# An attention and two-layer MoE kernel: another order of the opening's hand-written plan, and the first transposes in another PSUM bank

## The chip, the cores and the metric

The kernel runs on one core of a Trainium2 chip. The metric is the device time of one execution in microseconds (us), and the number quoted for a kernel is the median of its runs. Five engines matter: PE (matrix products, with PEld loading its weights), DVE and ACT (elementwise work, reductions and activations), POOL (hardly used), and SP, which issues the transfers (DMAs). Each engine works through its own instruction list strictly in the order in which the program wrote it; engines wait for each other through semaphores.

## The reference

```python
scores = scale * np.matmul(q_c, k_c.transpose(0, 1, 2, 4, 3))      # blocks of 64 tokens, 8 heads
attn = np.exp(scores - np.max(scores, axis=-1, keepdims=True))
attn = attn / (np.sum(attn, axis=-1, keepdims=True) + 1e-09)
x = (attn @ v_c), heads joined                                       # 2304 tokens x 512
h = x @ w_in;   g = h * (1.0 / (1.0 + np.exp(-1.702 * h)));          x = g @ w_out   # 512 -> 2048 -> 512
h = x @ w_in2;  g = h * np.tanh(log1p(exp(h)));                      return g @ w_out2
```

So there are three stages: chunked attention with a softmax over blocks of 64 keys, then two feed-forward layers. The weights arrive as 64-bit floats, and the kernel makes 32-bit numbers of them itself.

## The kernel before

**Tiling.** The 2304 tokens are 18 attention tiles of 128 tokens. Three tiles make a block of 384 tokens, and a block is what the first layer's in-projection takes as its moving operand. The hidden width of 2048 is cut into 16 steps of 128. Step n of a block has an in-projection, called `I` n here (`in_proj`, 12 matmuls of 128x384 into a bank `h`), a GELU on ACT, a split of its result into a high and a low part, and an out-projection, called `O` n (`out_a`, 12 matmuls into the banks `acc0` and `acc1`). Each product of 32-bit accuracy is three matmuls of rounded parts: high weight x high x, high weight x low x, low weight x high x (`mm3`, lines 354 to 356). The third matmul of a product therefore is the first that reads the low part of the weight.

**The weights of the first layer.** There are 32 weight tiles, numbered in the order of use: in-weights i0, i1, then o0, i2, o1, i3, o2, i4 and so on, so in-weight n is number 2n-1. During the first 16 steps each is loaded by SP and then converted in four operations on two engines: a scale on ACT (`c`, line 196), a join of the two 32-bit words on DVE (`j`, lines 200 and 201), a cast to the high part on ACT (`s`, line 155), and the subtraction that makes the low part on DVE (`rest`, line 163). In the second and later blocks the converted weights lie in memory and are used again.

**What sets the order.** The scheduler is switched off: instructions stand in each engine's list in the order in which the program emits them. For the first block's attention (tiles 0 to 2), the fourth tile's attention up to its normalisation, in-projections 0 to 3 and out-projections 0 and 1, a string of steps named `PLAN` (line 24) gives that order, one letter per step: `T` transposes of q and k, `Q K` copies out of PSUM, `S` scores, `M` maximum and subtraction, `X` exp, `N` sums, `U` normalisation, `A` transposes of the weights of attention, `V` its copy, `P` the product with v, `H L` the high and low part of x, `I` in-projection, `G Y Z` GELU and its parts, `O` out-projection, `l` a weight load, `d v` loads of tokens, `w` a number of idle matmuls that only keep PE busy, and `c j s` as above. After it a plain loop (line 748) runs from step 4. In each of its first 12 turns it emits a piece of a later tile's attention, the in-projection, a call of `convert`, the GELU and its high part, the out-projection of two steps back, and `convert` again. One `convert` (line 171) emits one cast, one join, the pending low parts and one scale, each for the next tile in line. The attention piece in turns 7 and 12 is scores, shift, exp, sums and normalisation. How far the conversions are ahead of the in-projections in the loop is set by how many of them `PLAN` holds.

**Banks.** `usual` and `every` (lines 619 and 620) are lists of PSUM tags that an attention tile takes in turn; the first three tiles go round `at`, `acc0` and `acc1`. The tag `h` has two buffers; the idle matmuls write one of them, and the in-projections then take them in turn.

Of the kernel before, what the change touches and what calls it, by code (L numbers as in the profile page):

```python
# [9 lines left out]
F32 = mybir.dt.float32  # L10
# [6 lines left out]
P = 128  # L17
# [4 lines left out]


PLAN = """
    w8 d0 d1 w8 T0 T1 w1 Q1 k0 K1 d2 q0 S0 M0 l S1 X0 T2 l v2 M1 N0 K2 l Q2 X1 S2 U0 c N1 c
    M2 j w17 l v0 A0 X2 N2 V0 c c j j v1 l U1 U2 A1 V1 P0 A2 d3 P1 s H0 V2 c w2 H1 s L0 P2 s
    T3 j H2 d4 K3 L1 Q3 s L2 c j I0 G0 s c j s S3 I1 Y0 G1 c Y1 Z0 M3 j Z1 c s c I2 G2 j s
    Y2 I3 c j O0 Z2 j X3 N3 s U3 s j G3 c s Y3 c O1 Z3 j
"""
BF16 = mybir.dt.bfloat16  # L30
PSUM = bass.MemoryType.PSUM
# [4 lines left out]
def tile_kernel(  # L36
# [17 lines left out]
    nc = tc.nc  # L54
# [18 lines left out]
    ident = const.tile([P, P], F32, name="ident")  # L73
# [9 lines left out]
    def wslot(tag, shape, dtype, name):  # L83
        pool = early_w if FREED.index(tag) < SOON else late_w
        return pool.tile(shape, dtype, tag=tag, name=name)


    class Weights:
# [54 lines left out]
        def join(self):  # L143
            if (i := self._next("join")) is None:
                return
            self.f32[i] = join_raw(self.raw.pop(i))

        def split(self):
            if (i := self._next("split")) is None:
                return  # L150
            key = kind, f = self.order[i]
            w = self.f32.pop(i)
            both = wslot(f"w{kind}{f}", [P, 2, DM], F32R, f"w{kind}{f}")
            hi, lo = both[:, 0], both[:, 1]
            nc.scalar.copy(hi, w)
            self.hi[key] = hi
            self.open.append((key, w, hi, lo))
# [72 lines left out]
    class Attention:  # L230
# [77 lines left out]
            rc = self.rc.to_broadcast([P, G, CH])  # L308
            eng.tensor_tensor(out=self.eg, in0=self.eg, in1=rc, op=ALU.mult)

        def attn_t(self):
            self.pt = self.psum("at")
            for p in range(NP):
                s = slice(p * P, (p + 1) * P)
                nc.tensor.transpose(self.pt[:, 0, s], self.e[:, s], ident)

        def take_a(self, copy):
            if self.a is None:
                self.a = at.tile([P, DM], F32, tag="k", name=f"a{self.i}")
            copy(self.a, self.pt[:, 0, :])  # L320

        def pv(self):
            self.pt = pt = self.psum("pv")
# [285 lines left out]
    ps = ctx.enter_context(tc.tile_pool(name="ps", bufs=2, space=PSUM))  # L609
# [7 lines left out]
    with tc.manual_schedule():  # L617
        at, ps_at = at_cm.__enter__(), ps_at_cm.__enter__()
# [7 lines left out]
        tiles = dict(enumerate(first))  # L626
# [4 lines left out]
        w1 = W[0]  # L631
# [26 lines left out]
        def join():  # L658
# [9 lines left out]
            "c": lambda _: w1.scale(),  # L668
            "j": lambda _: join(),
            "s": lambda _: split(),  # L670
            "T": lambda i: tiles[i].transposes(),
            "Q": lambda i: tiles[i].take("q", act),
            "K": lambda i: tiles[i].take("k", act),
# [4 lines left out]
            "X": lambda i: tiles[i].exp(),  # L678
            "N": lambda i: tiles[i].sums(),
            "U": lambda i: tiles[i].normalize(nc.vector),  # L680
            "A": lambda i: tiles[i].attn_t(),
            "V": lambda i: tiles[i].take_a(act),
            "P": lambda i: tiles[i].pv(),
            "H": lambda i: tiles[i].x_hi(act),
# [63 lines left out]
        for n in range(4, NA):  # L748
            f = n % KF
# [25 lines left out]
            j = n // KF  # L775
# [142 lines left out]
        G2 = {}  # L918
# [25 lines left out]
        for p in range(PAIRS):  # L944
# [78 lines left out]
            for i, (k, c) in enumerate(units):  # L1023
                name = OUT[k]
# [65 lines left out]
```

## Time and profile before

| what | value |
|---|---|
| median of 3 runs | 847.68 us (847.05 to 847.93) |
| the profiled execution | 848.96 us, of which the span is 847.1 us |
| PE busy | 826.9 us (98%), 6228 instructions |
| DVE busy | 551.8 us (65%), 1059 instructions |
| ACT busy | 394.3 us (47%), 710 instructions |
| DMA, q1 | 120064 packets, 179.33 MB, 66.6% |
| mean granted clock of PE | 0.995 |

The page's slices, 21 us each, show where PE is not full: 6 tenths in the first, 8 in the second, 9 or more in nearly all others. The chain that ended last is 85% PE. The shares of the other engines are averages; in the opening DVE (5, 7, 9, 8, 7 tenths) and ACT (3, 7, 9, 8, 6 tenths) are far busier than later. The profiled execution took 1.28 us more than the median of the runs, and its span ends 1.86 us short of its own time.

### The profile page before, as it was taken

The numbers are of one execution on the slowest core, as the hardware profiler recorded it, in microseconds if no ns is written. First come the engines' busy times: TensorE is split into PE (matmuls) and PEld (weight loads), VectorE is DVE, ScalarE is ACT, GpSimd is POOL, SyncE is SP. The second block draws the span as 40 slices with busy tenths as digits, with TensorE's granted clock in tenths as the row PEclk, the third lists the DMA queues.
The fourth block names the chain that finished last, engine by engine and source line by source line (L and its number), as shares of the span: only waits on it lengthen the run. The fifth ranks groups of instructions, "written<-read, shape, count | busy, mean of one in ns | idle before, by whom it ended". The sixth has DMA issues, their size and how long they took to land.

```text
span 847.1 us, 15662 instructions
## 1 busy us (share of the span) xinstructions
PE 826.9 (98%) x6228; PEld 804.9 (95%) x6228; DVE 551.8 (65%) x1059; ACT 394.3 (47%) x710; POOL 0.7 (0%) x6
## 2 busy tenths in 40 slices
PE   6899999999999999999999999999999999999998
PEld 4799899999999999999999999999999999999998
DVE  5798757657676766766525466678556687566664
ACT  3798644445544443545212333356333365333442
POOL 0000000000000000000000000000000000000000
PEclk9899999999999999999999999999999999999999
DMA  9867634747667673864445278788888778877761
GB/s 245 269 189 242 176 113 142 207 155 242 176 199 216 172 230 130 250 173 163 164 149 224 87 246 301 250 269 259 249 312 275 263 243 262 273 253 236 256 199 56
DMA packets 120135, 180.31 MB, mean 213 GB/s; under 512 B 61440, under 2 KB 82432, under 8 KB 120064
## 3 DMA queue, kind: packets, MB, share of 16 engines
q1 hardware_dynamic: 120064, 179.33, 66.6%
q8 instruction: 49, 0.80, 0.4%
q14 instruction: 22, 0.18, 0.1%
HBM read 140.51 MB, written 38.80 MB: 212 GB/s over the span
## 4 chain that ended last, share of the span: by engine, by line
PE 85%; DVE 7%; ACT 3%; DMA 3%; SPq 1%; issue 1%; DVEq 0%
PE sum_acc L887 14%; PE sum_y L857 11%; PE h L857 9%; PE h L354 7%; PE acc L355 7%; PE acc L356 7%; PE acc L354 7%; PE h L355 7%; PE h L356 7%; PE sum_y L887 5%; DMA raw<-in_moe_w_out_dram 1%; PE tr L258 1%; DVE raw L201 1%; PE sc L275 1%; PE pv L330 1%; SPq L224 1%
## 5 line engine op out<-in xcount | busy, mean ns | idle before, releaser
L354 PE MATMUL h<-xh,wi 128*128 128x384 f32 x384 | 134.9, 351 | 0.0
L355 PE MATMUL acc<-gl,wo 128*128 128x384 f32 x384 | 129.2, 337 | 1.8 <-DVE gl L380 1.8
L356 PE MATMUL h<-xh,wi 128*128 128x384 f32 x384 | 129.1, 336 | 1.8 <-DVE wi L163 1.8
L355 PE MATMUL h<-xl,wi 128*128 128x384 f32 x384 | 129.2, 336 | 0.5 <-DVE xl L350 0.5
L356 PE MATMUL acc<-gh,wo 128*128 128x384 f32 x384 | 129.1, 336 | 0.0
L354 PE MATMUL acc<-gh,wo 128*128 128x384 f32 x384 | 129.1, 336 | 0.0
L372 ACT ACTIVATE t<-h 128x384 f32<-128x384 f32 x96 | 47.0, 490 | 125.4 <-PE h L356 100.0
L376 DVE CAST gh<-t 128x384 fp32r<-128x384 f32 x80 | 28.8, 360 | 90.2 <-ACT t L372 90.2
L355 PEld LDWEIGHTS acc<-gl,wo 128*128 128x128 f32 x384 | 72.2, 188 | 2.4 <-DVE gl L380 2.4
L356 PEld LDWEIGHTS h<-xh,wi 128*128 128x128 f32 x384 | 72.2, 188 | 2.1 <-DVE wi L163 2.1
L354 PEld LDWEIGHTS h<-xh,wi 128*128 128x128 f32 x384 | 72.2, 188 | 2.0
L355 PEld LDWEIGHTS h<-xl,wi 128*128 128x128 f32 x384 | 72.4, 188 | 0.8 <-DVE xl L350 0.8
L356 PEld LDWEIGHTS acc<-gh,wo 128*128 128x128 f32 x384 | 72.2, 188 | 0.0
L354 PEld LDWEIGHTS acc<-gh,wo 128*128 128x128 f32 x384 | 72.2, 188 | 0.0
L380 DVE TENSOR_TENSOR gl<-t,gh 128x384 fp32r<-128x384 f32 x96 | 53.5, 557 | 5.5 <-ACT gh L376 2.7
L867 ACT ACTIVATE v<-h 128x384 f32<-128x384 f32 x24 | 11.9, 494 | 61.9 <-PE h L857 60.3
L926 DVE TENSOR_TENSOR v<-u,sum_y 128x384 f32<-128x384 f32 x24 | 13.3, 553 | 31.7 <-PE sum_y L857 31.7
L926 DVE TENSOR_TENSOR g_a<-u,sum_y 128x384 f32<-128x384 f32 x24 | 13.3, 553 | 31.0 <-PE sum_y L857 31.0
L867 ACT ACTIVATE g_a<-g_a 128x384 f32<-128x384 f32 x24 | 12.6, 525 | 40.8 <-DVE g_a L926 40.8
L867 ACT ACTIVATE v<-v 128x384 f32<-128x384 f32 x24 | 12.6, 524 | 35.2 <-DVE v L926 35.2
L926 DVE TENSOR_TENSOR g_s<-v,g_s 128x384 f32<-128x384 f32 x48 | 26.8, 558 | 0.8
L461 DVE TENSOR_TENSOR s<-raw2i,s 128x512 fp32r<-128x512 f32 (+1 forms) x32 | 19.9, 621 | 10.8 <-ACT s L460 10.8
(499 smaller groups left out, 1841.0 us busy)
## 6 DMA issues: line engine op xcount, KB each, us to landing
fs<-w_sums SPq DMA_DIRECT2D x84, 512.0 KB, 4.6
fb_p<-w_out_sums SPq DMA_DIRECT2D x60, 512.0 KB, 4.4
w_sums<-s SPq DMA_DIRECT2D x24, 512.0 KB, 2.6
fa<-w_outs SPq DMA_DIRECT2D x24, 512.0 KB, 4.7
raw<-in_moe_w_in_dram SPq DMA_DIRECT2D x16, 512.0 KB, 5.8
raw<-in_moe_w_out_dram SPq DMA_DIRECT2D x16, 512.0 KB, 5.5
raw2i<-in_moe_w_in_dram SPq DMA_DIRECT2D x16, 512.0 KB, 4.6
raw2o<-in_moe_w_out_dram SPq DMA_DIRECT2D x16, 512.0 KB, 5.2
```

The costliest lines, as they stand in the source:

```text
L201: nc.vector.scalar_tensor_tensor(hi, hi, 3, lo, op0=ALU.logical_shift_left, op1=ALU.bitwise_or)
L354: nc.tensor.matmul(o, wh, mh, start=start, stop=False)
L355: nc.tensor.matmul(o, wh, ml, start=False, stop=False)
L356: nc.tensor.matmul(o, wl, mh, start=False, stop=stop)
L372: nc.scalar.activation(gt[n], hp.pop(n), AF.Gelu_apprx_sigmoid)
L376: (nc.scalar.copy if n < KF else nc.vector.tensor_copy)(gh[n], gt[n])
L380: nc.vector.tensor_tensor(out=gl[n], in0=gt.pop(n), in1=gh[n].bitcast(F32), op=ALU.subtract)
L461: nc.vector.tensor_tensor(out=lo, in0=w, in1=hi.bitcast(F32), op=ALU.subtract)
L857: nc.tensor.matmul(h, t[:, u, which, ks], moving[:, kk], start=start and kk == 0 and i == 0, stop=kk == 1 and i == 2, skip_group_check=not ...
L867: nc.scalar.activation(t, c, AF.Mish)
L887: nc.tensor.matmul(o, gs[a][:, ts], w[:, b], start=start and i == 0 and t != 1, stop=stop and i == 2, skip_group_check=again or t > 0,)
L926: nc.vector.tensor_tensor(out=out, in0=x, in1=h, op=op)
```

## The change

The plan is written in another order, and three other edits come with it. The step `A` of the plan (tiles 0 to 2) no longer takes the next tag of its tile's list but a bank of the tag `h`, handed to it as an argument (the loop still calls it without one). A step `r` is new: it emits the pending low parts of weights. One `PLAN` line of each side stands for the string:

```diff
-    w8 d0 d1 w8 T0 T1 w1 Q1 k0 K1 d2 q0 S0 M0 l S1 X0 T2 l v2 M1 N0 K2 l Q2 X1 S2 U0 c N1 c
+    w8 d0 d1 w8 T0 T1 w1 Q1 k0 K1 d2 q0 S0 M0 l S1 X0 T2 v0 M1 N0 K2 l Q2 X1 S2 U0 v1 l v2
...
-        def attn_t(self):
-            self.pt = self.psum("at")
+        def attn_t(self, bank=None):
+            self.pt = self.psum("at")[:, 0, :] if bank is None else bank
             for p in range(NP):
                 s = slice(p * P, (p + 1) * P)
-                nc.tensor.transpose(self.pt[:, 0, s], self.e[:, s], ident)
+                nc.tensor.transpose(self.pt[:, s], self.e[:, s], ident)
...
-            copy(self.a, self.pt[:, 0, :])
+            copy(self.a, self.pt)
...
+            "r": lambda _: w1.rest(),
...
-            "A": lambda i: tiles[i].attn_t(),
+            "A": lambda i: tiles[i].attn_t(ps.tile([P, 512], F32, tag="h", name=f"at{i}")),
```

Counted in the two strings: before, 13 `c`, 12 `j` and 11 `s`; now 10, 9 and 8. All else is there equally often but for the idle matmuls, `l` (5, now 7) and `r` (none, now 1).

**PE, tiles 0 to 2 and the first in-projection.** `at` is the transposes of step `A`, `pv` step `P`, `tr3` the fourth tile's `T`, `h0` in-projection 0; rows of idle matmuls are left out. Before:

```order
L315 MATMUL at0_276<-ident_72,e0_172 128x128 x4
L315 MATMUL at1_301<-ident_72,e1_209 128x128 x4
L330 MATMUL pv0_308<-a0_287,v0_274 64x64 x16
L315 MATMUL at2_325<-ident_72,e_first_106 128x128 x4
L330 MATMUL pv1_336<-a1_306,v1_295 64x64 x16
...
L330 MATMUL pv2_384<-a_first_107,v2_207 64x64 x16
L258 MATMUL tr3_403<-ident_72,q3_330 128x128 x4
L258 MATMUL tr3_403<-ident_72,k3_332 128x128 x4
L354 MATMUL h0_439<-xh0_373,wi0_353 128x384
```

Now:

```order
L315 MATMUL at0_251<-ident_72,e0_172 128x128 x4
L330 MATMUL pv0_271<-a0_259,v0_205 64x64 x16
...
L315 MATMUL at1_294<-ident_72,e1_207 128x128 x4
L330 MATMUL pv1_319<-a1_307,v1_241 64x64 x16
...
L315 MATMUL at2_340<-ident_72,e_first_106 128x128 x4
L330 MATMUL pv2_350<-a_first_107,v2_245 64x64 x16
L354 MATMUL h0_394<-xh0_299,wi0_367 128x384
...
L258 MATMUL tr3_424<-ident_72,q3_313 128x128 x4
```

Each tile's `A` and `P` now stand together with idle matmuls between the tiles, and the fourth tile's transposes stand behind in-projection 0.

**DVE, from the fourth tile's shift on.** `e3`, `sm3` and `rc3` belong to that tile's softmax; `raw` with a number is a weight tile being joined, `wi` and `wo` with a step's number its low part. Before:

```order
L290 TENSOR_TENSOR e3_501<-sc3_462,mx3_502 128x512
L200 TENSOR_SCALAR raw6_357<-raw6_357 128x512
L201 SCALAR_TENSOR_TENSOR raw6_357<-raw6_357 128x512
L163 TENSOR_TENSOR wi3_460<-raw5_355,wi3_460 128x512
L380 TENSOR_TENSOR gl1_508<-t1_494,gh1_497 128x384
L200 TENSOR_SCALAR raw7_359<-raw7_359 128x512
L201 SCALAR_TENSOR_TENSOR raw7_359<-raw7_359 128x512
L163 TENSOR_TENSOR wo2_511<-raw6_357,wo2_511 128x512
L200 TENSOR_SCALAR raw8_361<-raw8_361 128x512
L201 SCALAR_TENSOR_TENSOR raw8_361<-raw8_361 128x512
L163 TENSOR_TENSOR wi4_532<-raw7_359,wi4_532 128x512
```

Now:

```order
L290 TENSOR_TENSOR e3_502<-sc3_468,mx3_503 128x512
L380 TENSOR_TENSOR gl1_506<-t1_464,gh1_499 128x384
L200 TENSOR_SCALAR raw4_311<-raw4_311 128x512
L201 SCALAR_TENSOR_TENSOR raw4_311<-raw4_311 128x512
L163 TENSOR_TENSOR wi2_466<-raw3_269,wi2_466 128x512
L303 TENSOR_REDUCE sm3_529<-e3_502 128x8
L304 TENSOR_SCALAR sm3_529<-sm3_529 128x8
L305 RECIPROCAL rc3_530<-sm3_529 128x8
L309 TENSOR_TENSOR e3_502<-e3_502,rc3_530 128x512
L200 TENSOR_SCALAR raw5_369<-raw5_369 128x512
L201 SCALAR_TENSOR_TENSOR raw5_369<-raw5_369 128x512
L163 TENSOR_TENSOR wo1_511<-raw4_311,wo1_511 128x512
```

Where the low parts of i3, o2 and i4 stood, those of i2 and o1 stand now, and the sums and the normalisation of the fourth tile have moved in front of the low part of o1.

**ACT, turn 7 of the loop.** `e4` is the exp of the fifth tile, `t7` and `gh7` the GELU of step 7 and its high part, `wi` and `wo` with a step's number the cast of that weight. Before:

```order
L298 ACT_TABLE_LOAD
L298 ACTIVATE e4_818<-e4_818 128x512
L155 CAST wi9_842<-raw17_665 128x512
L196 ACTIVATE raw19_733<-raw19_733 128x512
L372 ACT_TABLE_LOAD
L372 ACTIVATE t7_852<-h7_829 128x384
L376 CAST gh7_854<-t7_852 128x384
L155 CAST wo8_868<-raw18_707 128x512
```

Now:

```order
L298 ACT_TABLE_LOAD
L298 ACTIVATE e4_789<-e4_789 128x512
L155 CAST wo6_813<-raw14_390 128x512
L196 ACTIVATE raw16_704<-raw16_704 128x512
L372 ACT_TABLE_LOAD
L372 ACTIVATE t7_823<-h7_800 128x384
L376 CAST gh7_825<-t7_823 128x384
L155 CAST wi8_839<-raw15_462 128x512
```

The instructions are the same, but each conversion is that of a weight three places earlier: the cast behind `gh7` was that of o8 and is that of i8.

## Rows read from the trace of the kernel before

**Rows 1.** Busy time by stretch: length, busy of each engine (instructions), PEclk, DMA, GB/s.
```profile
100.00:200.00 100.00, 100.00 (x814) 97.19 (x813) 62.72 (x129) 46.19 (x77) 0.00 (x0) 1.00 0.55 165
200.00:400.00 200.00, 200.00 (x1626) 194.37 (x1625) 136.80 (x285) 95.95 (x161) 0.00 (x0) 1.00 0.63 189
```

**Rows 2.** Timeline of PE, opening: start, duration, instruction, [idle before <-releaser].
```profile
21.34 1.09 PE L315 MATMUL at<-ident,e 128*128 128x128 f32 x4 [4.71 <-DVE e L309]
...
28.42 0.42 PE L354 MATMUL h<-xh,wi 128*128 128x384 f32 x1
29.38 0.45 PE L355 MATMUL h<-xl,wi 128*128 128x384 f32 x1 [0.54 <-DVE xl L350]
...
38.71 0.44 PE L356 MATMUL h<-xh,wi 128*128 128x384 f32 x1 [1.82 <-DVE wi L163]
...
45.90 0.63 PE L315 MATMUL at<-ident,e 128*128 128x128 f32 x4 [1.02 <-DVE e L309]
...
46.72 0.34 PE L356 MATMUL h<-xh,wi 128*128 128x384 f32 x1
```

**Rows 3.** Timeline of PE, in-projections 7 and 8, and two later waits.
```profile
60.67 0.69 PE L275 MATMUL sc<-kt,qt 64*64 64x64 f32 x32
61.29 0.44 PE L354 MATMUL h<-xh,wi 128*128 128x384 f32 x1
...
65.56 0.34 PE L354 MATMUL h<-xh,wi 128*128 128x384 f32 x1
...
68.51 0.44 PE L355 MATMUL acc<-gl,wo 128*128 128x384 f32 x1 [0.54 <-DVE gl L380]
...
93.84 0.44 PE L355 MATMUL acc<-gl,wo 128*128 128x384 f32 x1 [1.27 <-DVE gl L380]
```

**Rows 4.** Stretches of 1 us around PE's long gap; PEclk is the granted clock.
```profile
19.00:20.00 1.00, 0.00 (x0) 0.00 (x0) 0.90 (x3) 0.00 (x0) 0.00 (x0) 0.96 0.95 342
20.00:21.00 1.00, 0.00 (x0) 0.00 (x0) 1.00 (x2) 0.00 (x0) 0.00 (x0) 0.50 1.05 296
26.00:27.00 1.00, 1.00 (x34) 0.72 (x32) 0.69 (x2) 1.00 (x3) 0.00 (x0) 0.63 0.97 206
```

**Rows 5.** Timeline of DVE: the first normalisation.
```profile
13.24 0.69 DVE L309 TENSOR_TENSOR e<-e,rc 128x512 f32<-128x512 f32 x1
```

**Rows 6.** Timeline of DVE behind the fifth tile's scores.
```profile
62.35 0.68 DVE L289 TENSOR_REDUCE mx<-sc 128x8 f32<-128x512 f32 x1
...
64.46 0.69 DVE L303 TENSOR_REDUCE sm<-e 128x8 f32<-128x512 f32 x1 [0.70 <-ACT e L298]
...
66.24 0.42 DVE L200 TENSOR_SCALAR raw<-raw 128x512 int32<-128x512 int32 x1
...
67.30 0.68 DVE L163 TENSOR_TENSOR wi<-raw,wi 128x512 fp32r<-128x512 f32 x1
...
69.51 0.68 DVE L163 TENSOR_TENSOR wo<-raw,wo 128x512 fp32r<-128x512 f32 x1
```

**Rows 7.** Timeline of ACT behind the fifth tile's scores.
```profile
63.80 0.63 ACT L298 ACTIVATE e<-e 128x512 f32<-128x512 f32 x1 [0.78 <-DVE e L290]
...
65.56 1.28 ACT L372 ACT_TABLE_LOAD   x1
66.86 0.49 ACT L372 ACTIVATE t<-h 128x384 f32<-128x384 f32 x1
67.38 0.52 ACT L376 CAST gh<-t 128x384 fp32r<-128x384 f32 x1
67.80 0.65 ACT L155 CAST wo<-raw 128x512 fp32r<-128x512 f32 x1
```

**Rows 8.** Timeline of ACT: a copy, and a scale that waited for its load.
```profile
11.50 0.58 ACT L264 COPY kt<-tr 128x512 f32<-128x512 f32 x1
...
18.26 0.68 ACT L196 ACTIVATE raw<-raw 128x512 f32<-128x512 f32 x1 [0.31 <-DMA raw<-in_moe_w_in_dram]
```

**Rows 9.** Timeline of SP: the fourth tile's load of k.
```profile
23.59 0.37 SPq L224 DMA_DIRECT2D k<-in_k_dram  x1
```

More of the change, by code (lines that the diff above doesn't have):

```diff
@@ L24 @@
 PLAN = """
-    w8 d0 d1 w8 T0 T1 w1 Q1 k0 K1 d2 q0 S0 M0 l S1 X0 T2 l v2 M1 N0 K2 l Q2 X1 S2 U0 c N1 c
-    M2 j w17 l v0 A0 X2 N2 V0 c c j j v1 l U1 U2 A1 V1 P0 A2 d3 P1 s H0 V2 c w2 H1 s L0 P2 s
-    T3 j H2 d4 K3 L1 Q3 s L2 c j I0 G0 s c j s S3 I1 Y0 G1 c Y1 Z0 M3 j Z1 c s c I2 G2 j s
-    Y2 I3 c j O0 Z2 j X3 N3 s U3 s j G3 c s Y3 c O1 Z3 j
+    w8 d0 d1 w8 T0 T1 w1 Q1 k0 K1 d2 q0 S0 M0 l S1 X0 T2 v0 M1 N0 K2 l Q2 X1 S2 U0 v1 l v2
+    w4 A0 M2 V0 c N1 X2 U1 l P0 w6 A1 H0 N2 V1 c U2 l d3 P1 w4 A2 H1 j L0 V2 P2 s L1 r H2 l
+    c L2 I0 j s d4 c j T3 I1 G0 s c Y0 K3 j Q3 Z0 l G1 s S3 O0 Y1 c M3 Z1 j s I2 X3 G2 N3
+    U3 c Y2 j s Z2 O1 c j s I3 G3 Y3 c j Z3 s c j
 """
```

## The prediction

> **What bounds the kernel now.** I read the busy time by stretch first. From 100 to 400 us PE is busy in every microsecond [rows 1], so whatever is lost or won before 100 us arrives at the end unchanged; the order of the instructions from turn 16 of the loop on is not touched. I then read PE's timeline in the opening for its gaps. Before the first in-projection matmul at 28.42 PE stands idle for 4.71 us; after it, up to the third matmul of in-projection 4 at 46.72, it waits three times, 0.54 + 1.82 + 1.02 = 3.38 us, each time for DVE [rows 2]. Up to in-projection 15 it waits twice more, 0.54 and 1.27 us, again for DVE [rows 3]. So the opening is bound first by the softmax chain of the first three tiles, and then by the conversion of weights on ACT and DVE. The granted clock fell inside the long gap: a mean of 0.96 in the stretch from 19 to 20 us puts the fall at 19.92, 3.3 us after the last matmul (21.34 - 4.71 = 16.63), and 0.63 from 26 to 27 puts the return at 26.74 [rows 4]. Between them PE ran at 1.2 GHz.
>
> **Part one: the way to in-projection 0.** Until the first normalisation ends, at 13.24 + 0.69 = 13.93 [rows 5], both orders are alike. Then I walk the new order with these durations: a DVE operation on 512 columns 0.69 (the next starts 0.61 later, or 0.72 if it needs the result), sums and normalisation together 1.78 from start to next start (64.46 to 66.24), a join 1.06 and a low part 0.60 from start to start [rows 6]; on ACT exp 0.63, cast 0.65, GELU 0.49, its high part 0.52, table load 1.28 [rows 7], copy 0.58, scale 0.68 [rows 8], each next start about 0.09 before the end; on PE four transposes 0.6, the small products of a tile 0.69, an in- or out-projection 2.1 ((65.56 - 61.29) / 2) [rows 2, 3]; about 0.05 from engine to engine.
>
> DVE goes on without a wait: shift of tile 2 to 15.25, tile 1 normalised at 17.0, tile 2 at 18.8, join of i0 to 19.8. PE transposes tile 1 from 17.05 to 17.65, ACT copies it by 18.3, PE multiplies with v by 19.0, ACT takes the high part by 19.65; then tile 2: transposes 19.7 to 20.3, copy 20.9, product 21.65, high part 22.3, low part on DVE 23.0. In-projection 0 starts at 22.3, where it started at 28.42, and its second matmul, which needs that low part, at 23.0. So it comes 6.1 us earlier, and with gaps of about 1 us on PE in place of 4.71 I let the clock stay at 2.4 GHz. The loads allow it: the first eight behind q and k are the same as before in another order, the one of them that ACT waited for last had landed at 18.26 [rows 8], where the walk wants i2 at 24.7 and the last v at 20.9, and the fourth tile's k, issued at 23.59 behind the release of tile 0's buffer [rows 9], is now free at about 16. Moving three sets of transposes into the bank `h` costs nothing by itself: their readers are done by 20.9, before in-projection 0 asks for a buffer. If that cover failed, the wait would be one copy, 0.6.
>
> **Part two: from there to in-projection 4.** Now ACT is full. Scale of o0 22.9; join of i1 22.95 to 24.1; cast of i1 24.8; scale of i2, table load and GELU 0 to 27.05; cast of o0, scale of o1, high part of GELU 0 to 28.65; two copies for the fourth tile to 29.6. Only then can its scores start: PE waits about 1.6. Scores end at 30.35, shift on DVE at 31.8, then gl1, join of o1 to 33.35 and the low part of i2 to 33.95; in-projection 2 reads it in its third matmul, due at 32.75: a wait of 1.2. ACT casts o1 after that join (34.05), loads the exp table (35.25), exp to 35.9. DVE normalises to 37.75, joins i3 (38.8), and writes the low part of o1 by 39.4; out-projection 1 wants it at 36.05: a wait of 3.35. In-projection 3 then runs to 43.3, GELU 3 to 44.0, its high part 44.5, scale 45.15, cast of i4 45.7; the low part of i4 comes at 46.8 behind gl3 and the join of o3. The third matmul of in-projection 4 starts at 46.85, where it started at 46.72: +0.1. The head start of 6.1 is used up by the fourth tile's transposes, now behind the start (0.9), and by waits of about 0.6 + 1.6 + 1.2 + 3.35 + 2.75 where there were 3.38.
>
> The new waits are not in the trace, so I bound this term. From below: no wait behind the start, 23.0 - 0.7 + (46.72 - 28.42 - 3.38) + 0.9 = 38.1, which is 8.6 earlier. From above: transposes and small products at the half clock, 0.49 (1.09 against 0.6) and about as much for each of the six, 2.9 later. I take the walk, +0.1, since each step in it is a row.
>
> **Part three: the loop.** At its entry the plan had done 11 casts and has now done 8. In-projection 4 reads weight tile number 7, the eighth: the lead of three tiles is gone, and each turn's second `convert` casts just the in-weight that the next in-projection reads. In most turns that is in time: from the end of an in-projection GELU, high part and cast take about 1.65, and PE has an out-projection of 2.1 to do. In turns 7 and 12 the exp stands before it. From the start of the maximum to the end of the second low part DVE took 69.51 + 0.68 - 62.35 = 7.84 [rows 6]; from the same start to the end of the cast behind the high part ACT took 67.80 + 0.65 - 62.35 = 6.10 [rows 7]. These two chains had weights with room; now they carry i8 and i13. The scores end at 60.67 + 0.69 = 61.36 [rows 3]; with DVE free (in this row it came 1 us late, which would only add) the cast ends at 61.43 + 6.10 = 67.53 and the low part at 61.43 + 7.84 = 69.27. PE has two projections meanwhile and wants them at 65.56 and 65.91: 2.0 for the first, 1.4 more for the second, 3.36 together. Twice, 6.72; the waits of 0.54 and 1.27, which the same softmax caused, are contained in it. Part three: 6.72 - 1.81 = +4.9. Its bounds: 0 less 1.81 if the casts were early enough, and 2 x (3.36 + 0.99) - 1.81 = +6.9 with DVE as late as it was.
>
> **Sum.** 0.1 + 4.9 = +5.0 on the span of 847.1; the profiled execution of 848.96 becomes 853.96. The median lies 1.28 below that execution, so the median becomes 852.7.
>
> One page gives another price for the table load between exp and GELU. In the trace the GELU starts 66.86 - 65.56 = 1.30 after the load's start, 0.02 after its end [rows 7]. "ScalarE: Activation LUTs" of the Trainium skill, section "What ACT_TABLE_LOAD costs", has 1283 ns for the load and another 1380 ns of drain for each switch. The load agrees, the drain is not in this row; with it each chain would be 1.38 longer and the sum 855.4, an estimate by that page. I keep the row and give this price no chance of its own, since the row shows the same load in the same place.
>
> **Rivals.** *The clock falls.* In the 3.35 us before the third matmul of out-projection 1 PE does nothing, and the clock fell 3.3 us into the one gap shown. It would then run at 1.2 GHz for some 26.74 - 21.34 = 5.4 us of work, which loses 2.7 us; the wait at in-projection 4 hangs on the end of in-projection 3 and hides none of it: 855.4. For it: the gap is as long. Against: it is no longer than that one, and before it PE is dense. "TensorE: Matmul & The Clock Gate" of the Trainium skill, section "What's actually happening", has the same two levels, with the lower one following an idle stretch; the rows agree.
>
> *DVE's throughput decides, not the chain.* DVE's work is the same, and in the trace it hardly pauses; if the last weights came at the same time as before, PE would reach turn 15 at the same time: 847.7. Against: a wait that begins at the scores and ends at the next in-projection leaves DVE idle in each round, and idle time is not made up.
>
> *The conversions keep up.* Faster, if the head start survives the opening. The place is the third matmul of out-projection 1, the price the 8.6 of the lower bound: 847.7 - 8.6 + 4.9 = 844.0. It decides for this side if that matmul starts before about 36, the point at which PE itself is ready. For it: loads now come early. Against: on ACT and DVE nearly every microsecond from 22 to 35 is taken.
>
> **Chances.** Forecast 0.58, clock 0.22, same pace 0.12, keeping up 0.08. The first two are slower, so 0.80 slower, 0.12 within 0.2% (1.7 us, about what a measurement of this kernel can tell from no change), 0.08 faster. The likeliest alone has 850.5 to 855.0. With the clock above and the fringe of the even case below, the range is 849.0 to 857.0.
>
> **What would show it.** Right: in-projection 0 starts near 22.3; PE waits for ACT at the fourth tile's scores, and for DVE `wo` L163 in out-projection 1 for some 3 us; in-projections 8 and 13 each begin with a wait for a cast of `wi` (about 2) and one for its low part (about 1.4); PEclk stays at 1.00 from 13 to 50; PE is full from about 110 on. Wrong: no wait for `wi` in front of in-projections 8 and 13, or in-projection 4 well before 45 or after 48.

## The result, and the profile after

The changed kernel takes 859.91 us (median of 4 runs, 857.67 to 860.37) against 847.8 us for the kernel before beside it (4 runs): a ratio of 1.0136, 95% interval 1.0124 to 1.0148. It is slower, as forecast, but by 12.1 us and not by 5.0, and the time lies outside the range. The profiled execution took 859.97 us with a span of 858.1.

The timeline of PE in the changed kernel, opening first (columns as in [rows 2]; the number in brackets is idle time before the instruction):

```profile
22.17 0.44 PE L354 MATMUL h<-xh,wi 128*128 128x384 f32 x1 [0.70 <-ACT xh L346]
22.89 0.44 PE L355 MATMUL h<-xl,wi 128*128 128x384 f32 x1 [0.29 <-DVE xl L350]
...
29.53 0.69 PE L275 MATMUL sc<-kt,qt 64*64 64x64 f32 x32 [1.49 <-ACT qt L264]
...
33.90 0.44 PE L356 MATMUL h<-xh,wi 128*128 128x384 f32 x1 [1.05 <-DVE wi L163]
...
39.48 0.44 PE L356 MATMUL acc<-gh,wo 128*128 128x384 f32 x1 [3.23 <-DVE wo L163]
...
45.85 0.44 PE L354 MATMUL h<-xh,wi 128*128 128x384 f32 x1 [1.80 <-ACT wi L155]
...
47.07 0.45 PE L356 MATMUL h<-xh,wi 128*128 128x384 f32 x1 [0.60 <-DVE wi L163]
...
67.41 0.34 PE L356 MATMUL acc<-gh,wo 128*128 128x384 f32 x1
69.60 0.44 PE L354 MATMUL h<-xh,wi 128*128 128x384 f32 x1 [1.85 <-ACT wi L155]
69.88 0.34 PE L355 MATMUL h<-xl,wi 128*128 128x384 f32 x1
71.35 0.44 PE L356 MATMUL h<-xh,wi 128*128 128x384 f32 x1 [1.13 <-DVE wi L163]
...
98.50 0.45 PE L354 MATMUL h<-xh,wi 128*128 128x384 f32 x1 [1.85 <-ACT wi L155]
...
100.24 0.69 PE L356 MATMUL h<-xh,wi 128*128 128x384 f32 x1 [1.12 <-DVE wi L163]
...
112.21 0.45 PE L354 MATMUL h<-xh,wi 128*128 128x384 f32 x1
```

In-projection 15 in the kernel before:

```profile
101.16 0.45 PE L354 MATMUL h<-xh,wi 128*128 128x384 f32 x1
```

The 4.71 us gap of [rows 2] is gone, and in-projection 0 starts 6.3 us earlier. Then come the fourth tile's scores, in-projection 2, out-projection 1 and in-projection 4, each with the wait the prediction named, and in-projections 8 and 13 (69.60, 98.50) with a wait for a cast and one for a low part, where [rows 3] had 0.54 and 1.27. In-projection 15 starts at 112.21 where it started at 101.16: 11.05 later, and the spans differ by 11.0. From there on nothing is lost, as [rows 1] led one to expect.

The chain behind the fifth tile's scores in the changed kernel, DVE and then ACT:

```profile
63.46 0.69 DVE L289 TENSOR_REDUCE mx<-sc 128x8 f32<-128x512 f32 x1 [0.28 <-PE sc L275]
...
70.61 0.69 DVE L163 TENSOR_TENSOR wi<-raw,wi 128x512 fp32r<-128x512 f32 x1
```
```profile
68.90 0.65 ACT L155 CAST wi<-raw 128x512 fp32r<-128x512 f32 x1
```

From the maximum's start to the end of the low part it is 70.61 + 0.69 - 63.46 = 7.84 us, to the end of the cast 68.90 + 0.65 - 63.46 = 6.09. [rows 6, 7] gave 7.84 and 6.10. The chain is the same; it now carries weights that are wanted at once.

The queue of SP, the fourth tile's load of k, now 6.8 us earlier than in [rows 9]:

```profile
16.77 1.84 SPq L224 DMA_DIRECT2D k<-in_k_dram  x1
```

What the forecast put at nothing, and one rival priced in another place, is the clock. Stretches of 1 us of the changed kernel; PEclk is the third number from the right, as in [rows 4]:

```profile
48.00:49.00 1.00, 1.00 (x6) 1.00 (x5) 1.00 (x3) 0.00 (x0) 0.00 (x0) 0.59 0.00 0
51.00:52.00 1.00, 1.00 (x6) 1.00 (x5) 0.60 (x1) 0.98 (x2) 0.00 (x0) 0.70 0.00 0
72.00:73.00 1.00, 1.00 (x5) 1.00 (x4) 1.00 (x3) 0.00 (x0) 0.00 (x0) 0.54 0.65 135
75.00:76.00 1.00, 1.00 (x6) 1.00 (x6) 0.00 (x0) 1.00 (x3) 0.00 (x0) 0.75 0.79 264
99.00:100.00 1.00, 0.12 (x1) 0.00 (x0) 1.00 (x2) 0.41 (x2) 0.00 (x0) 0.69 0.65 189
106.00:107.00 1.00, 1.00 (x8) 0.96 (x7) 0.90 (x3) 0.03 (x1) 0.00 (x0) 0.89 0.00 0
```

Between the two lines of each pair the clock is at 0.50, that is 1.2 GHz. Such a time is called a low stretch here, and its start a fall. Taken to the tenth, as the prediction did with [rows 4], the low stretches are 48.2 to 51.6, 72.1 to 75.5 and 99.4 to 106.2: 3.4, 3.4 and 6.8 us. Each begins in or behind the waits at in-projections 4, 8 and 13. In the first two PE had been at work again since 47.07 and 71.35 when the clock fell; the third begins inside the second wait of in-projection 13, which ends at 100.24. The trace has none at the 3.23 us wait in out-projection 1, the only place where a rival had put one.

### The profile page after: what moved, and what is told of

It is laid out like the page before. It is cut to its first block, busy times and chain, and to the rows that moved or that the text cites. A ratio compares the mean times of both kernels' runs of the same rounds, so it can differ in the third digit from the quotient of the medians.

```text
span 858.1 us, 15654 instructions
## 1 busy us (share of the span) xinstructions
PE 830.2 (97%) x6223; PEld 808.1 (94%) x6223; DVE 553.0 (64%) x1059; ACT 395.3 (46%) x710; POOL 0.7 (0%) x6
## 4 chain that ended last, share of the span: by engine, by line
PE 90%; DVE 6%; ACT 3%; DMA 1%; issue 0%; SPq 0%; DVEq 0%
PE sum_acc L888 14%; PE sum_y L858 11%; PE h L858 9%; PE h L354 8%; PE acc L356 8%; PE acc L354 8%; PE h L356 8%; PE acc L355 8%; PE h L355 7%; PE sum_y L888 5%; PE tr L258 2%; PE pv L330 1%; PE sc L275 1%; PE at L315 1%; DVE g_s L927 1%; DVE raw L201 1%
## 5 line engine op out<-in xcount | busy, mean ns | idle before, releaser
L354 PE MATMUL h<-xh,wi 128*128 128x384 f32 x384 | 136.3, 355 | 6.2 <-ACT wi L155 5.5
L356 PE MATMUL h<-xh,wi 128*128 128x384 f32 x384 | 131.1, 341 | 3.9 <-DVE wi L163 3.9
L354 PEld LDWEIGHTS h<-xh,wi 128*128 128x128 f32 x384 | 73.0, 190 | 9.2 <-ACT wi L155 6.4
L356 PEld LDWEIGHTS h<-xh,wi 128*128 128x128 f32 x384 | 73.2, 191 | 5.3 <-DVE wi L163 5.2
L356 PEld LDWEIGHTS acc<-gh,wo 128*128 128x128 f32 x384 | 73.1, 190 | 3.6 <-DVE wo L163 3.6
L354 PEld LDWEIGHTS acc<-gh,wo 128*128 128x128 f32 x384 | 73.4, 191 | 0.1
```

The costliest lines, as they stand in the source:

```text
L354: nc.tensor.matmul(o, wh, mh, start=start, stop=False)
L356: nc.tensor.matmul(o, wl, mh, start=False, stop=stop)
```

## The experiments

Twelve microseconds have three candidates: the lost lead (how many weight tiles the conversions are ahead of the projections when the loop starts), the new bank, the clock. The lead comes first, then the bank, then the clock in both kernels, and at the end lead and clock together.

**The lead taken from the old order (x2).** The kernel before, without the last three scale-join-split rounds of its order:

```diff
-    Y2 I3 c j O0 Z2 j X3 N3 s U3 s j G3 c s Y3 c O1 Z3 j
+    Y2 I3 j O0 Z2 X3 N3 U3 G3 Y3 O1 Z3
```

> The kernel before, with its old order of the opening, but with the last three scales, joins and casts of the plan left out, so that it enters the loop with 10, 9 and 8 of them as the changed kernel does; the loop does them later. Theory A: waits of about 2.0 and 1.3 us for cast and low part of the in-weight appear at in-projections 8 and 13, with a stretch at 1.2 GHz behind each, at the end +4 to +5 for the waits and +3 to +5 for the clock: 855 to 857.5 us. Theory B: the lead does not matter, 847 to 849 us.

Measured: 855.73 us (852.97 to 856.9), ratio to before 1.0081, interval 1.0057 to 1.0105. PE in this kernel:

```profile
66.92 0.44 PE L354 MATMUL h<-xh,wi 128*128 128x384 f32 x1 [1.85 <-ACT wi L155]
68.68 0.69 PE L356 MATMUL h<-xh,wi 128*128 128x384 f32 x1 [1.14 <-DVE wi L163]
...
95.64 0.45 PE L354 MATMUL h<-xh,wi 128*128 128x384 f32 x1 [1.85 <-ACT wi L155]
```

The same waits of 1.85 and 1.14 us at the same two in-projections, in the old opening with the old banks. So the mechanism of part three holds: it is the lead that keeps the softmax of turns 7 and 12 off PE's path.

**The lead given back inside the loop (x1).** The changed kernel with a third conversion in turns 4, 5 and 6:

```diff
+                if n in (4, 5, 6):
+                    W[0].convert()
```

> The changed kernel with one call of the conversion more in each of turns 4, 5 and 6 of the loop, so that the three weight tiles which the new plan leaves over are caught up before turn 7. Theory A (the lost lead makes the waits at in-projections 8 and 13, and the clock falls behind these waits): both waits for the cast of the in-weight (1.85 us each) and its low part (1.1) go, and so do the two stretches at 1.2 GHz near 72 and 99 us (about 3.4 and 6.8 us long); the wait at in-projection 4 and its low-clock stretch stay. Gain 4.9 + 4.7 us less 1 to 3 us for crowding on DVE in turns 6 and 7, where the old waits for gl (0.5 and 1.3) come back: 851 to 853 us. Theory B (the new opening and the bank cost the time, the loop's waits only follow from it): under 2 us gained, 858 to 860 us.

Measured: 854.49 (853.97 to 856.34), ratio 1.0075, interval 1.0054 to 1.0095. The waits for `wi` at 8 and 13 are gone, and the gain stays short of 851 to 853, since the extra conversions crowd DVE:

```profile
47.98 0.44 PE L354 MATMUL h<-xh,wi 128*128 128x384 f32 x1 [1.82 <-ACT wi L155]
...
74.33 0.44 PE L355 MATMUL acc<-gl,wo 128*128 128x384 f32 x1 [3.77 <-DVE gl L380]
```

In-projection 4 still waits, because the lead is rebuilt only after it, and out-projection 6 waits 3.77 us for a low part of GELU that stands behind the added work on DVE. Three low stretches of the clock are in its trace too.

**The lead given back in the order (x5).** The changed kernel, whose opening up to in-projection 3 stays as it is; two more rounds stand behind that. They give back two of the three tiles of lead, though the expectation calls the lead as large as before: the plan has 12 `c`, 11 `j` and 10 `s` now, one of each less than before the change.

```diff
-    U3 c Y2 j s Z2 O1 c j s I3 G3 Y3 c j Z3 s c j
+    U3 c Y2 j s Z2 O1 c j s I3 c j s c j G3 Y3 s c Z3 j s c j
```

> The changed kernel with the order's last four steps written longer: two more scale-join-split rounds stand between in-projection 3 and the end, so that the lead of weight tiles that the loop starts with is as large as before the change (the opening up to in-projection 3 is the new one, untouched). Theory A (the waits at in-projections 8 and 13 come from the lost lead, and each wait in the opening lets the clock fall once): no wait for wi in front of 8 and 13, the wait at in-projection 4 down from 2.4 us to under 1, the waits at the fourth tile's scores (1.5) and in out-projection 1 (3.2) unchanged; two low stretches of the clock at most, before 60; 847 to 851 us. Theory B (the softmax of the new opening is itself the loss, whatever the lead): in-projection 4 still comes after 47, 856 or more.

Measured: 848.41 (846.2 to 850.73, 11 runs), ratio 1.0002, interval 0.9990 to 1.0013: from 12 us slower to even. No wait for `wi` is left at 8, 13 or 4; the third matmul of in-projection 4 starts at 46.23 with no idle time before it. Two low stretches are left in the profiled execution:

```profile
23.00:24.00 1.00, 0.79 (x3) 0.77 (x4) 0.97 (x3) 0.00 (x0) 0.00 (x0) 0.73 0.80 188
26.00:27.00 1.00, 1.00 (x5) 0.91 (x5) 0.90 (x2) 0.90 (x2) 0.00 (x0) 0.57 0.96 321
40.00:41.00 1.00, 1.00 (x5) 1.00 (x6) 0.96 (x3) 0.56 (x1) 0.00 (x0) 0.76 1.32 158
43.00:44.00 1.00, 1.00 (x5) 1.00 (x4) 1.00 (x3) 0.79 (x2) 0.00 (x0) 0.53 0.83 176
```

PE in the same execution:

```profile
30.00 0.69 PE L275 MATMUL sc<-kt,qt 64*64 64x64 f32 x32
...
39.95 0.44 PE L356 MATMUL acc<-gh,wo 128*128 128x384 f32 x1 [3.23 <-DVE wo L163]
...
46.23 0.34 PE L356 MATMUL h<-xh,wi 128*128 128x384 f32 x1
```

The second starts 0.6 us after the matmul that ends the 3.2 us wait in out-projection 1. Here, then, the clock does fall at the place of the rival, with the same wait before it as in the changed kernel, where it did not. The first lies ahead of the fourth tile's scores, and it costs next to nothing: in-projection 0 starts 0.32 later than in the changed kernel (22.49 against 22.17) and the scores 0.47 later, without the wait of 1.49. PE, being slower, only uses up a wait that would have come. The expectation, which left that wait standing, missed this.

**The old banks (x4).** The changed kernel, with `A` taking the next tag of its tile's list again:

```diff
-            "A": lambda i: tiles[i].attn_t(ps.tile([P, 512], F32, tag="h", name=f"at{i}")),
+            "A": lambda i: tiles[i].attn_t(),
```

> The changed kernel with its new order, but the transposes of step A take the next tag of their tile's list again, as before. Theory A: the bank is no part of the loss; one more wait of about 0.9 us for tile 2's transposes at 20 us moves everything behind it by that much: 860 to 861.5 us. Theory B with the bank as its cause: 852 to 856 us.

Measured: 862.37 (861.29 to 863.02), ratio 1.0163, interval 1.0148 to 1.0178. This is above both ranges. The bank is a help: without it tile 2's transposes wait 0.59 us for a low part of x (`at` at 20.65) and in-projection 0 starts 1.2 us later (23.38). The other half of the 2.5 us is not split further here: the trace has five low stretches where there were three.

**The clock held up in the loop only (x3).** The changed kernel with matmuls on zeros, which compute nothing that is used, before in-projections 8 and 13:

```diff
+            if n in (8, 13):
+                warm = ps_at.tile([P, 2, 512], F32, tag="at", name=f"warm{n}", bufs=1)
+                for _ in range(18):
+                    nc.tensor.matmul(warm[:, 0, 0:TB], zeros[:, 0:P], zeros, start=True, stop=True)
```

> The changed kernel with 18 idle matmuls (about 3.1 us at the full clock) put in front of in-projections 8 and 13, where PE waits anyway; nothing else differs. Theory A says that the waits cost 4.9 us and the clock behind them 1.7 and 3.0 us: the waits stay (PE is now busy in them), the clock stays at 2.4 GHz behind both, 859.9 - 4.7 = 855 us. If the low clock costs nothing, because the engines that feed PE are behind anyway: 859 to 860 us. If the matmuls come at a bad place and delay the in-projections: 860 to 862 us.

Measured: 856.64 (856.14 to 857.93), ratio 1.0099, interval 1.0083 to 1.0114. The low stretches behind 72 and 99 are gone, but the opening now has two, and the time stays above the 855 of Theory A:

```profile
39.00:40.00 1.00, 0.39 (x1) 0.40 (x2) 1.00 (x3) 1.00 (x2) 0.00 (x0) 0.54 1.31 172
42.00:43.00 1.00, 1.00 (x6) 1.00 (x6) 0.90 (x3) 0.00 (x0) 0.00 (x0) 0.75 0.96 169
49.00:50.00 1.00, 1.00 (x6) 1.00 (x5) 1.00 (x2) 0.40 (x1) 0.00 (x0) 0.67 0.00 0
52.00:53.00 1.00, 1.00 (x5) 1.00 (x5) 0.00 (x1) 1.00 (x3) 0.00 (x0) 0.63 0.00 0
```

One of them is at the wait in out-projection 1. Which of its waits an execution pays for differs between these executions, so a test of the clock has to fill all of them.

**The clock held up in all long waits (x8).** Two new letters, `b` and `e`, give so many matmuls on zeros into the banks `at` and `acc1`:

```diff
-    c L2 I0 j s d4 c j T3 I1 G0 s c Y0 K3 j Q3 Z0 l G1 s S3 O0 Y1 c M3 Z1 j s I2 X3 G2 N3
-    U3 c Y2 j s Z2 O1 c j s I3 G3 Y3 c j Z3 s c j
+    c L2 I0 j s d4 c j T3 I1 G0 s c Y0 K3 j Q3 Z0 l G1 s e8 S3 O0 Y1 c M3 Z1 j s I2 X3 G2 N3
+    U3 c Y2 j s Z2 b18 O1 c j s I3 G3 Y3 c j Z3 s c j b10
...
+            if n in {8: 16, 13: 16}:
+                warm({8: 16, 13: 16}[n], ps_at, "at")
```

> The changed kernel with matmuls on zeros, which compute nothing that is used, in each long wait: 8 before the fourth tile's scores, 18 before out-projection 1, 10 before in-projection 4, 16 each before in-projections 8 and 13. The waits for weights stay as they are; only PE is not idle in them. Theory A (what the prediction missed, 6 us, is the clock's three falls behind the waits): no low stretch from 13 us on, the five waits still set the pace, so 852 to 854.5, the figure of the walk without the clock. Theory B (the falls are a bystander, and the 6 us lie in slower ACT and DVE work or contention): 857 or more, with the clock at 1.00 all the same.

Measured: 854.64 (854.25 to 856.43, 5 runs), ratio 1.0083, interval 1.0070 to 1.0095. That is just above Theory A's range. The profiled execution is the 854.64 itself, with a span of 852.4. Two stretches of this kernel, and then of the changed kernel:

```profile
13.00:60.00 47.00, 41.80 (x388) 34.32 (x381) 36.73 (x69) 34.22 (x59) 0.00 (x0) 1.00 0.75 215
60.00:110.00 50.00, 48.71 (x397) 44.43 (x396) 41.85 (x77) 39.48 (x67) 0.00 (x0) 1.00 0.79 218
```
```profile
13.00:60.00 47.00, 35.74 (x340) 31.11 (x336) 35.44 (x66) 32.64 (x56) 0.00 (x0) 0.96 0.73 207
60.00:110.00 50.00, 44.05 (x312) 41.68 (x312) 38.67 (x72) 36.72 (x62) 0.00 (x0) 0.90 0.74 212
```

PEclk is 1.00 throughout where it was 0.96 and 0.90, and the time drops by 5.3 us, though PE has 68 matmuls more to do. The weights still set the pace, as the third matmuls of in-projections 4, 8 and 13 and the first of 15 show:

```profile
47.13 0.44 PE L356 MATMUL h<-xh,wi 128*128 128x384 f32 x1 [0.57 <-DVE wi L163]
...
69.85 0.44 PE L356 MATMUL h<-xh,wi 128*128 128x384 f32 x1 [0.65 <-DVE wi L163]
...
97.17 0.45 PE L356 MATMUL h<-xh,wi 128*128 128x384 f32 x1 [0.64 <-DVE wi L163]
...
106.41 0.45 PE L354 MATMUL h<-xh,wi 128*128 128x384 f32 x1
```

In the changed kernel these start at 47.07, 71.35, 100.24 and 112.21. Up to the first fall the two kernels agree to 0.06 us; each of the first two low stretches then costs 1.6 us, and the long one 2.7. Of the five runs three have a mean clock of 0.999 and take 854.25 to 854.64, two have 0.997 and take 856.33 and 856.43: about 2 us. A stretch of 3.4 us at half speed would lower the mean by as much (an estimate: 3.4 x 0.5 / 854 = 0.002); these two runs have no trace.

**The same, opening only (x11).** Without the matmuls before in-projections 8 and 13:

```diff
-            if n in {8: 16, 13: 16}:
-                warm({8: 16, 13: 16}[n], ps_at, "at")
```

> The kernel of x8 without the matmuls on zeros before in-projections 8 and 13; those in the three waits of the opening stay. Splits the price of the falls. Theory A (each wait of 3 us in the loop lets the clock fall, for 3.4 us or twice that): no low stretch before 60, one behind 72 and one behind 99 in most runs; 1.6 for a short one and 3.2 for a long one over the 854.6 of x8: 857 to 859.5. Theory B (the falls of the loop came only because the clock had fallen shortly before): none, 854.6.

Measured: 858.25 (858.15 to 858.53), ratio 1.0120, interval 1.0105 to 1.0135.

```profile
13.00:60.00 47.00, 41.84 (x403) 34.27 (x392) 36.66 (x69) 34.09 (x60) 0.00 (x0) 1.00 0.74 212
60.00:110.00 50.00, 44.14 (x313) 41.53 (x311) 38.81 (x73) 37.02 (x62) 0.00 (x0) 0.90 0.75 210
```

The opening has none, the loop has its two. They cost 858.25 - 854.64 = 3.6 us together; the one of the opening costs 859.91 - 858.25 = 1.7, with intervals that overlap. The traces of the changed kernel and of x8, above, have 1.6 for the one of the opening and 4.3 for the two of the loop.

**The kernel before with its own gap filled (x7, then x10).** 24 more matmuls on zeros in the gap of 4.71 us:

```diff
-    M2 j w17 l v0 A0 X2 N2 V0 c c j j v1 l U1 U2 A1 V1 P0 A2 d3 P1 s H0 V2 c w2 H1 s L0 P2 s
+    M2 j w17 l v0 A0 w24 X2 N2 V0 c c j j v1 l U1 U2 A1 V1 P0 A2 d3 P1 s H0 V2 c w2 H1 s L0 P2 s
```

> The kernel before, with 24 matmuls on zeros more in the 4.71 us gap in front of the second set of transposes. They compute nothing that is used. Theory A (a fall of the clock costs what the work in the low stretch loses): no fall between 13 and 30 us, the span shorter by the 1 to 1.5 us that the transposes, the small products and the first in-projection lost at half speed; 846 to 847 us. Theory B (the clock falls by time or by load, not by idleness of PE): the fall stays or comes elsewhere, no gain, 847.7 or more.

Measured: 847.53 (845.88 to 848.38), ratio 0.9991, interval 0.9983 to 1.0000. The fall of [rows 4] is gone, and another comes at 28.9, behind waits of 0.82 us for k and 1.09 us for a low part of x, so the median is only 0.6 us below the 848.09 of the kernel before beside it. A second filling in front of the fourth tile's transposes, matmuls on zeros into the bank `at`, takes it away:

```diff
-    T3 j H2 d4 K3 L1 Q3 s L2 c j I0 G0 s c j s S3 I1 Y0 G1 c Y1 Z0 M3 j Z1 c s c I2 G2 j s
+    b4 T3 j H2 d4 K3 L1 Q3 s L2 c j I0 G0 s c j s S3 I1 Y0 G1 c Y1 Z0 M3 j Z1 c s c I2 G2 j s
```

> The kernel of x7 with 4 matmuls on zeros more before the fourth tile's transposes, which waited 0.82 us for k ahead of the one fall that was left. Theory A: no fall in most runs, 846 to 847, 0.5 to 1 less than x7. Theory B (the next wait, 1.09 us in front of the second matmul of in-projection 0, is enough for a fall, and the number of falls is chance): falls as in x7, 847.5.

Measured: 846.81 (846.43 to 847.6, 11 runs), ratio 0.9987, interval 0.9978 to 0.9995. The stretches from 13 to 60 and from 60 to 110 in this kernel:

```profile
13.00:60.00 47.00, 42.48 (x418) 36.36 (x419) 41.46 (x79) 37.48 (x67) 0.00 (x0) 1.00 0.87 247
60.00:110.00 50.00, 48.73 (x369) 46.66 (x368) 38.52 (x72) 36.13 (x62) 0.00 (x0) 1.00 0.67 185
```

PEclk is 1.00 from 13 to 110. This is the kernel before without its clock losses, to set beside the 854.64 above.

**Lead and clock together (x9).** The kernel of x5, with the lead in its order, and `e3`, `b3`, `b4`, `e8` and `b18` in its waits:

```diff
-    A0 M2 V0 c N1 X2 U1 l P0 w6 A1 H0 N2 V1 c U2 l d3 P1 w4 A2 H1 j L0 V2 P2 s L1 r H2 l
-    c L2 I0 j s d4 c j T3 I1 G0 s c Y0 K3 j Q3 Z0 l G1 s S3 O0 Y1 c M3 Z1 j s I2 X3
-    G2 N3 U3 c Y2 j s Z2 O1 c j s I3 c j s c j G3 Y3 s c Z3 j s c j
+    A0 M2 V0 c N1 X2 U1 l P0 w6 A1 H0 N2 e3 V1 c U2 l d3 P1 w4 A2 H1 j L0 b3 V2 P2 s L1 r H2 l
+    c L2 b4 I0 j s d4 c j T3 I1 G0 s c Y0 K3 j Q3 Z0 l G1 s e8 S3 O0 Y1 c M3 Z1 j s I2 X3
+    G2 N3 U3 c Y2 j s Z2 b18 O1 c j s I3 c j s c j G3 Y3 s c Z3 j s c j
```

> The kernel of x5 (new opening, the lead of weight tiles built in the order) with matmuls on zeros, which compute nothing that is used, in its waits: 3 each before the small products with v of tiles 1 and 2, 4 before in-projection 0, 8 before the fourth tile's scores, 18 before out-projection 1. Theory A (lead and clock together are all that the change lost): neither waits for wi at 8 and 13 nor a low stretch of the clock from 13 to 110 us; in-projection 15 at or before 100 us where it started at 101.16 before the change, time 845.5 to 847, the lowest of all kernels here. Theory B (the falls are not tied to idle PE): low stretches all the same, 848 or more.

Measured: 846.47 (846.14 to 847.23, 12 runs), ratio 0.9981, interval 0.9972 to 0.9989: faster than both kernels, and 1.35 us below the one before.

```profile
13.00:60.00 47.00, 43.47 (x434) 35.86 (x430) 40.28 (x78) 37.66 (x66) 0.00 (x0) 1.00 0.83 233
60.00:110.00 50.00, 49.57 (x403) 47.77 (x395) 40.17 (x76) 37.14 (x63) 0.00 (x0) 1.00 0.70 201
```
```profile
98.88 0.45 PE L354 MATMUL h<-xh,wi 128*128 128x384 f32 x1
```

PE is busy 49.57 of the 50 us from 60 on, and in-projection 15 starts at 98.88, 2.28 earlier than before the change. The 12 runs lie within 1.1 us, those of the kernel before, on the same chip, within 3.1 (23 runs).

**The account.** With the medians of the kernels in which the clock stays up, the 12.1 us divide into three parts: clock losses of the changed kernel 859.91 - 854.64 = 5.3, less those of the kernel before, 847.82 - 846.81 = 1.0; the lost lead 854.64 - 846.47 = 8.2; all the rest of the new order 846.47 - 846.81 = -0.3. Their sum is 12.1 (the second and third are differences of kernels that also differ in their fillings; the kernel before had medians of 847.80 to 848.09 beside these runs, so a part is known to about 0.3 us). The 8.2 are what two of the three tiles bring. About 2.0 of them lie at in-projection 4: from out-projection 1's third matmul to in-projection 4's it is 47.13 - 39.52 = 7.61 us in x8 and 45.70 - 40.08 = 5.62 in x9. The rest are the waits at 8 and 13. So the lost lead also cost time at the end of the opening, where the early start of in-projection 0 was used up.

## Why the prediction was right in direction and wrong in size

- **Way to in-projection 0: right.** 22.3 and 23.0 predicted, 22.17 and 22.89 found; the clock stayed at 2.4 GHz there. The fourth tile's k is issued at 16.77 (its buffer free at about 16 predicted), against 23.59 in [rows 9].
- **The waits up to in-projection 4: right.** About 1.6, 1.2, 3.35 and 2.75 predicted; 1.49, 1.05, 3.23 and 1.80 + 0.60 found as idle time. The prediction counts from when a matmul is due. Matmuls in a row start 0.17 us apart but are shown as 0.34 long, so the idle time shown is 0.17 shorter; counted the prediction's way the first three are 1.66, 1.22 and 3.40. The third matmul of in-projection 4 is at 47.07, predicted 46.85. The prediction's list of what used up the head start comes to +0.9 (9.5 + 0.9 - 3.38 - 6.1), not to the +0.1 of its walk, in part because it mixes the two ways; the forecast went by the walk.
- **The waits in the loop: right in place, cause and size.** 3.36 a time predicted. Counted the same way, in-projection 8 waits 69.60 - 67.41 - 0.17 = 2.02 and then 71.35 - 69.88 - 0.17 = 1.30, together 3.32. (The 1.81 taken off for the old waits was idle time as shown; counted alike it is 2.14.) Taking the lead out of the old order makes the same waits appear, putting two of its three tiles back into the new one makes them go.
- **The sum without the clock: right.** With the clock held up the changed kernel has a span of 852.4, 5.3 over the 847.1 of the profile before; the sum said 5.0. Up to in-projection 4 it is +0.4 (47.13 against 46.72; 0.1 predicted), from there to in-projection 15 +4.8 (4.9 predicted).
- **The clock: wrong, and this is the step that failed.** The prediction let the clock stay at 2.4 GHz in all that follows ("PEclk stays at 1.00 from 13 to 50"), and its rival "the clock falls" knew one place, the 3.35 us before out-projection 1, and one price, 2.7 us. The waits that the sum itself contains at in-projections 4, 8 and 13, 2.75 and twice 3.36 us, the latter as long as the one that the rival priced, were given no fall and no reason for that. Each is two shorter waits with 0.6 us of work between them, and in or behind each of them the clock fell. The three falls cost 5.3 us: 1.7 in the opening, 3.6 in the loop. The range ended at 857.0, with room for one fall and not for three. The argument against the rival, that the gap is no longer than the one in [rows 4] and that PE is dense before it, does not decide: with the same gap the clock fell in x5 and not in the changed kernel. So that the clock stayed up there, as forecast, is luck.
- **The step from the execution to the median: wrong by 1.3.** The 1.28 us by which the profiled execution of the kernel before stood above its median was taken off the changed kernel as well. The profiled execution after, 859.97, is 0.06 from its median. The one before, 848.96, lies inside the spread of its kernel, 846.91 to 850.01 in the 23 runs beside x9; why it was longer than the three beside it stays open.

Of the 7.2 us between forecast and result, 5.3 are the falls, 1.3 the median, 0.3 the walk, and 0.4 what lies around the span (2.24 in the kernel with the clock held up, 1.86 in the profile before). The rival of the even pace falls with this: DVE and ACT do the same work (553.0 us busy against 551.8, and 395.3 against 394.3), and the idle time in each softmax round is not made up. So does the rival of the faster side, since out-projection 1 starts its third matmul at 39.48 and not before 36.

## What to carry to other kernels

When a planned order is shortened at one end, count what it leaves in stock at the seam: two of three weight tiles of lead, invisible as a wait before, were worth 8 us. When a sum contains new waits of PE of about 3 us, price each at its own length and, besides, at a possible stretch at the lower clock behind it (here 5.3 us for three falls), less the waits that such a stretch runs into; two waits with 0.6 us of work between them were followed by a fall as a single one was. And set a forecast for the median on the runs, not on the one profiled execution.

## What the runs showed of the hardware that was not expected

- The clock fell when PE was already at work again: in the changed kernel at 48.2 and 72.1, PE having resumed with waits behind it at 47.07 and 71.35; in x5 at 40.5, PE having resumed at 39.95. In the changed kernel PEclk is 1.00 in each microsecond from 45 to 48, in which PE waits 1.80 and 0.60 us; the fall comes behind them. So a gap in which the clock stays at 1.00 is no proof that it costs nothing.
- The same wait need not be followed by a fall: the 3.23 us in out-projection 1 had one behind them in x5 and none in the changed kernel; in x2 the waits of 1.85 and about 1.1 us had one at in-projection 8 (at 68.2) and none at in-projection 13.
- A low stretch cost less where it lay in or ahead of a wait. The three in the changed kernel cost 1.6, 1.6 and 2.7 us, where half of their lengths, the loss of an engine that is never idle (an estimate), is 1.7, 1.7 and 3.4; the last begins inside a wait. The first one in x5, ahead of a wait, cost about 0.2.
- The same kernel pays differently from run to run: five runs of x8 had a mean clock of 0.999 or 0.997 and differed by 2 us accordingly. "TensorE: Matmul & The Clock Gate" of the Trainium skill, section "What's actually happening", says that one kernel shows 6, 11 or 14 slow matmuls at its start from run to run; these runs agree in kind, with the difference away from the start.
- Matmuls on zeros in the waits cost no time that shows: from the last matmul before the wait at in-projection 8 to its third it is 71.35 - 67.41 = 3.94 us without them and 69.85 - 65.91 = 3.94 with 16 of them. They narrow the spread: 1.1 us over the 12 runs of x9, against 4.5 over the 11 of x5, the same kernel without them on another chip.
